# Making pp @ w_in of chunks 2 to 7 one batch at a time, split by ScalarE and VectorE from PSUM

## The chip, the cores and the metric

The kernel runs on one core of a Trainium2 chip. The time is the device time of one execution in microseconds, the median of several runs. A second, profiled execution is read for the reasons; its own time is given beside the runs.

## What is computed

Four batches of 8 heads with 576 rows go through an attention over 32 packed rows, and its result (2304 rows of 512) through two feed-forward stages. q, k, v and p are float32; the weights arrive as float64 and are converted to float32 on the chip.

```python
p_packed = sm_attn(p, k, v)                  # 32 rows per head
out = sm_attn(q, p_packed, p_packed)         # 576 rows per head
x = out as (4*576, 512)
h = x @ w_in;  g = softplus(h);  y = g @ w_out          # d_ff = 2048
z = (sigmoid(y @ w_gate) * (y @ w_val)) @ w_out2        # d_ff = 1536
```

## The kernel before

The attention's second product and the first feed-forward product are joined: a2 (the 576 x 32 softmax of q against the packed rows, per head) times the packed rows pp times w_in is a2 @ (pp @ w_in). So for each batch b and each chunk c of 256 columns of w_in the kernel makes Wp[b, c] = pp @ w_in once, a matrix of 256 x 256 (as 128 partitions x 2 x 256), and then multiplies a2 with it. There are 8 chunks and 4 batches.

Products of full precision are made in two parts: hi is a float32 rounded to the format that TensorE multiplies fast, lo is the remainder x - hi. `mm3` multiplies hi x hi, hi x lo and lo x hi. So every operand has to be split: a copy to hi (`hi_of`, on ScalarE or GpSimd) and a subtraction for lo (`split_lo`, on VectorE or GpSimd). Wp is split into tiles wph and wpl.

For each (b, c) and each half s of the 576 rows, `emit_h` makes h in twelve matmuls of 288 columns into PSUM (lines 111 to 113), ScalarE makes softplus of it (g, L634), the split gives ghl, and two steps later `emit_out1` multiplies it with w_out: four blocks m of six matmuls each (L662, L663, L665), each block into a PSUM bank of its own, which VectorE adds into xa (L670). Chunks 0 and 1 are done batch by batch beside the attention; from chunk 2 on the entries go in pairs of batches (0, 1) and (2, 3).

Preparations are generators in a queue, `jobs`. Between two blocks m a `tick` runs the first job up to its next `yield`. So a job with many yields is spread over many blocks, and what stands behind it in the queue comes later. The queue holds, for each pair of batches, the job that makes the next pair's Wp, and behind it the conversions of w_in and w_out for a later chunk (`prep_win`, `prep_wo`), one early operand of the second stage, and near the end the operands A and B of the second stage (`prep_A`, `prep_B`). `finish` runs the queue until a named job is done. The framework then orders the instructions of each engine.

Wp is made by two functions. `prep_wp_one(b, c)` serves chunks 0 and 1: for one batch four matmuls with 64 columns of bdT (the packed rows as a block-diagonal matrix) as weights, each into one half of the partitions of a bank; ScalarE copies the bank to wph and VectorE subtracts into wpl; one yield. `prep_wp_two(half, c)` serves chunks 2 to 7: for two batches two times two matmuls with 128 columns of bdT. Each of its two banks holds one half of the partitions of both batches, so ScalarE copies it in two halves into float32 tiles of the pool cv (L598), and GpSimd then makes wph (L102) and wpl (L99). For the first pair alone (chunk 2, batches 0 and 1) ScalarE and VectorE split from PSUM in halves (L601). The job has ten yields (eight for the first pair).

The banks of `bank1` come from a pool of four, shared by the blocks of `emit_out1`, the sets of Wp and the conversions.

Of the kernel before, what the change touches and what calls it, by code (L numbers as in the profile page):

```python
# [12 lines left out]
AF = mybir.ActivationFunctionType  # L13
# [7 lines left out]
def attn_moe_moe_kernel(  # L21
# [21 lines left out]
    nc = tc.nc  # L43
# [45 lines left out]
    def bank1():  # L89
        return ps_o[-1].tile([P, 512], F32, tag="o", name="ps1")  # L90
# [7 lines left out]
    def split_lo(eng, lo, x, hi):  # L98
        eng.tensor_tensor(lo, x, hi.bitcast(F32), op=ALU.subtract)  # L99

    def pool_hi(hi, x):
        nc.gpsimd.tensor_scalar(hi, x, 1.0, 0.0, op0=ALU.mult, op1=ALU.add)  # L102

    def hi_of(on_act, hi, x):
        if on_act:
            nc.scalar.activation(hi, x, AF.Copy)  # L106
        else:
            pool_hi(hi, x)
# [23 lines left out]
    for c in range(NCH1):  # L132
        order += [("in", c, f) for f in range(2)] + [("out", c, f) for f in range(2)]
        if c > ECS:
            n = -(-len(early) // (NCH1 - c))
# [110 lines left out]
    jobs = deque()  # L246
# [3 lines left out]
    def tick():  # L250
        for todo_ in (jobs, idle):
            while todo_:
                if next(todo_[0][1], "end") != "end":
                    return
                todo_.popleft()

    def finish(name):
        while any(nm == name for nm, _ in jobs):
            tick()
# [6 lines left out]
    bdT = ph1.tile([P, 2 * B + 2, P], F32, name="bdT")  # L266
# [19 lines left out]

    BLANK = 2
    NWORK = 7
    WPP = 1
    WPH = 0  # L290
    SPL = []
    SP0 = []
    ALO = [['A22'], ['A22', 'S2', 'S4'], ['A22'], ['A22']]
# [214 lines left out]
    def att_left(u):  # L508

        return sum(STAGES - n for _, n, x in live if x <= u) + STAGES * sum(  # L510
            x <= u for x in units
        )

    def att_done(u):
        return att_left(u) == 0
# [6 lines left out]
    def att_tick(last=2 * B):  # L522

        if units and ready(units[0], 0) and units[0] <= last and (
            not live or (len(live) < (NLV if last < 8 else 2) and min(x[1] for x in live) >= (G0 if len(live) == 1 and last < 8 else GP if last < 8 else GAP))
        ):
            u = units.popleft()
            live.append([attn_unit(u), 0, u])
        for x in live:
            if ready(x[2], x[1]):  # L530
                live.remove(x)
                next(x[0])
                x[1] += 1
                if x[1] < STAGES:
                    live.append(x)
                return


    w_in_f, wo_hl, Wp = {}, {}, {}
# [6 lines left out]
    def prep_win(c):  # L546
        wt = ph1.tile([P, KD, CF], F32, tag="w_in", bufs=2, name="w_in")
        for f in range(2):
            yield from convert(("in", c, f), wt[:, :, f * P : (f + 1) * P])
            yield  # L550
        w_in_f[c] = wt

    def prep_wo(c):
        for f in range(2):
            wo_hl[c, f] = yield from convert_split(("out", c, f), wo_p, [P, DM], "wo", 4)
            yield

    def wp_tiles():
        return [
            ph1.tile([P, 2, CF], F32R, tag="wp" + y, bufs=4, name="wp" + y) for y in "hl"  # L560
        ]

    def prep_wp_one(b, c):
        half, odd = divmod(b, 2)
        wt = w_in_f[c]
        hi, lo = wp_tiles()
        ps = bank1().rearrange("p (t n) -> p t n", t=2)
        for t in range(2):
            for par in range(2):
                r = slice(64 * (odd ^ par), 64 * (odd ^ par) + 64)  # L570
                nc.tensor.matmul(
                    ps[r, t, :], bdT[:, 4 * half + 2 * t + par, r], wt[:, 2 * t + par, :],
                    start=True, stop=True,
                )
        nc.scalar.activation(hi, ps, AF.Copy)
        split_lo(nc.vector, lo, ps, hi)
        Wp[b, c] = (hi, lo)
        yield

    def prep_wp_two(half, c):  # L580
        wt = w_in_f[c]
        hl = [wp_tiles() for _ in range(2)]

        far = WPP and (half, c) != (0, 2)
        if far:
            xs = [new_cv().rearrange("p (t n) -> p t n", t=2) for _ in range(2)]
        for par in range(2):
            ps = bank1().rearrange("p (t n) -> p t n", t=2)
            for t in range(2):
                j = 2 * t + par  # L590
                nc.tensor.matmul(  # L591
                    ps[:, t, :], bdT[:, 4 * half + j, :], wt[:, j, :], start=True, stop=True
                )
            yield
            for e in range(2):
                r = slice(64 * e, 64 * e + 64)
                if far:
                    nc.scalar.activation(xs[e ^ par][r], ps[r], AF.Copy)  # L598
                else:
                    hi, lo = hl[e ^ par]  # L600
                    nc.scalar.activation(hi[r], ps[r], AF.Copy)  # L601
                    split_lo(nc.vector, lo[r], ps[r], hi[r])
                yield
            yield
        if far:
            for (hi, lo), x in zip(hl, xs):
                hi_of(WPH, hi, x)
                split_lo(nc.gpsimd, lo, x, hi)
                yield
        for x in range(2):  # L610
            Wp[2 * half + x, c] = hl[x]

    gt, late = {}, deque()

    def split_g(b, c, s, g32):
# [57 lines left out]
    def between(m, att_ticks):  # L673
        if m == LATE and late:
            late.popleft()()
        if m > 0:
            for _ in range(att_ticks[m - 1]):
                att_tick()
        tick()
# [90 lines left out]
    def new_cv():  # L770
        return cv.tile([P, DM], F32, tag="cv", name="cv")
# [41 lines left out]
    def prep_early(fs):  # L813
        for f in fs:
            yield from blocks(f)
            yield
# [31 lines left out]
    n = 0  # L848
# [19 lines left out]
    for i, (b, c) in enumerate(entries):  # L868
        if c == 0:
            while not att_done(2 * b + 1):  # L870
                att_tick()
            if b:
                for cc in range(2):
                    jobs.appendleft((f"wp{b}{1 - cc}", prep_wp_one(b, 1 - cc)))
        if (b, c) == (3, 0):
            jobs.append(("win2", prep_win(2)))
        if (b, c) == (3, 1):
            jobs.append(("wp02", prep_wp_two(0, 2)))
        if c >= 2 and b % 2 == 0:
            k = groups.index((b // 2, c))  # L880
            if k == 0:
                jobs.append(("wo2", prep_wo(2)))
            if k + 1 < len(groups):
                x, cc = groups[k + 1]
                jobs.append((f"wp{2 * x}{cc}", prep_wp_two(x, cc)))
            if k + 2 < len(groups) and weights and groups[k + 2][1] == weights[0]:
                cc = weights.popleft()
                jobs.extend(idle)
                idle.clear()
                jobs.append((f"win{cc}", prep_win(cc)))  # L890
                jobs.append((f"wo{cc}", prep_wo(cc)))
                idle.append((f"early{cc}", prep_early(early_in.get(cc, ()))))
            if (b, c) == BAT:
                jobs.extend(idle)
                idle.clear()
                jobs.append(("B00", prep_B(0, 0)))
        for x in range(2):
            if (b, c) == (x + 2, NCH1 - 2):
                jobs.append((f"A{x}", prep_A(x)))
        if (b, c) == CPC:  # L900
            cps[0] = CPS > 0
        if (b, c) == (1, 2):
            att.release()
            w2.append(tc.alloc_tile_pool(name="w2", bufs=1, side="right"))
        finish(f"wp{b}{c}" if c < 2 else f"wp{b - b % 2}{c}")
        for s in range(2):
            emit_h(b, c, s)
            pace = 0
            for bb in range(b + 1, B if c < 2 else 0):
                slots = 3 * (4 * bb - 2 * i - s) - MARGIN  # L910
                pace = max(pace, -(-att_left(2 * bb + 1) // max(1, slots)))
            ticks = [pace] * 3
            if len(pend) == DEPTH:
                emit_out1(*pend.popleft(), ticks)
            else:
                for m in range(KD):
                    between(m, ticks)
            pend.append((b, c, s))
# [176 lines left out]
```

## Time and profile before

| | us |
|---|---|
| median of 3 runs | 866.27 (866.12 to 866.31) |
| profiled execution, its own time | 866.7 |
| its span | 864.9 |
| TensorE busy | 840.2 |
| VectorE busy | 586.3 |
| GpSimd busy | 475.3 |
| ScalarE busy | 340.0 |

A page of the profile names engines as PE (TensorE matmul), PEld (TensorE weight load), DVE (VectorE), ACT (ScalarE), POOL (GpSimd) and SP (the queue of DMAs). Matmuls are pipelined: a record's duration is longer than the distance to the next one, so the cost of a matmul is read from the distance between starts. A matmul in float32 that isn't split, as those of Wp, leaves two records.

### The profile page before, as it was taken

The page shows a single profiled execution, that of the slowest core. Times are in us where ns is not written, and L with a number is a line of the kernel's source. Part 1 is how long each engine was busy: PE and PEld are TensorE (multiplying, and loading weights), DVE is VectorE, ACT ScalarE, POOL GpSimd, SP SyncE. Part 2 cuts the span into 40 slices and gives each one's busy share as a digit, 9 for nine tenths or more (in the row PEclk, how much of TensorE's full clock was granted, in tenths as well). Part 3 has the DMA queues.
Part 4 walks back from the last instruction along what each step waited for, and adds up shares of the span by engine and source line. Part 5 has one row for each costly group of instructions (what it writes and reads, how often), then busy time and mean ns, then how long its engine had stood idle before and what let it go on. Part 6 is the DMA issues. An engine that isn't in the chain of part 4 may idle for free.

```text
span 864.9 us, 15497 instructions
## 1 busy us (share of the span) xinstructions
PE 840.2 (97%) x6100; PEld 790.1 (91%) x6100; DVE 586.3 (68%) x1003; ACT 340.0 (39%) x626; POOL 475.3 (55%) x453
## 2 busy tenths in 40 slices
PE   6899999999999999999889999999999999999997
PEld 5788999899999999999889999999988999999995
DVE  1876556946465556546788688898896746767665
ACT  4567565554343434454333431232352432322210
POOL 4454333245656545585669787876983734536400
PEclk9999999999999999999999999999999999999999
DMA  9993330203033302300064555644415413213003
GB/s 230 221 223 89 83 80 5 88 11 99 5 96 103 123 25 77 125 26 1 1 198 148 166 168 153 192 129 131 161 56 153 113 47 86 67 44 110 14 1 109
DMA packets 58007, 85.53 MB, mean 99 GB/s; under 512 B 6352, under 2 KB 39248, under 8 KB 57936
## 3 DMA queue, kind: packets, MB, share of 16 engines
q1 hardware_dynamic: 56928, 83.31, 34.3%
q10 hardware_dynamic: 1008, 1.25, 0.4%
q8 instruction: 48, 0.79, 0.4%
q14 instruction: 23, 0.19, 0.1%
HBM read 65.67 MB, written 18.87 MB: 98 GB/s over the span
## 4 chain that ended last, share of the span: by engine, by line
PE 79%; DVE 8%; DMA 6%; ACT 2%; POOL 2%; issue 2%; SPq 0%; POOLq 0%; DVEq 0%; ACTq 0%
PE bank L113 9%; PE bank L111 8%; PE bank L112 8%; PE ps L662 7%; PE ps L663 6%; PE ps L665 6%; PE ps L1010 5%; PE ps L1012 5%; PE ps L1011 5%; PE ps L111 4%; PE ps L113 3%; PE ps L112 3%; DMA xa<-in_k_dram 2%; PE ps L591 2%; PE ps L466 1%
## 5 line engine op out<-in xcount | busy, mean ns | idle before, releaser
L111 PE MATMUL bank<-aop,BH 128*128 128x288 f32 x672 | 199.0, 296 | 4.3 <-ACT work L992 1.1
L113 PE MATMUL bank<-aop,BL 128*128 128x288 f32 x672 | 198.7, 296 | 0.0
L112 PE MATMUL bank<-aop,BH 128*128 128x288 f32 x672 | 197.8, 294 | 0.2 <-DVE aop L99 0.2
L670 DVE TENSOR_TENSOR xa<-xa,ps 128x288 f32<-128x288 f32 x224 | 100.2, 452 | 104.9 <-PE ps L665 104.5
L99 POOL TENSOR_TENSOR ghl<-g,ghl 128x576 fp32r<-128x576 f32 x64 | 93.3, 1458 | 134.2 <-ACT ghl L106 124.8
L662 PE MATMUL ps<-ghl,woh 128*128 128x288 f32 x512 | 148.7, 305 | 2.9 <-DVE xa L670 2.6
L663 PE MATMUL ps<-ghl,wol 128*128 128x288 f32 x512 | 143.4, 295 | 0.0
L111 PEld LDWEIGHTS bank<-aop,BH 128*128 128x128 f32 x672 | 126.2, 188 | 9.9 <-issue 2.1
L112 PEld LDWEIGHTS bank<-aop,BH 128*128 128x128 f32 x672 | 126.4, 188 | 4.2 <-DVE aop L99 0.4
L113 PEld LDWEIGHTS bank<-aop,BL 128*128 128x128 f32 x672 | 126.5, 188 | 0.1
L99 POOL TENSOR_TENSOR BL<-cv,BH 128x512 fp32r<-128x512 f32 (+1 forms) x96 | 118.3, 1249 | 3.5 <-ACT BH L106 2.4
L665 PE MATMUL ps<-ghl,woh 128*128 128x288 f32 x512 | 108.9, 294 | 0.0
L662 PEld LDWEIGHTS ps<-ghl,woh 128*128 128x128 f32 x512 | 96.2, 188 | 5.7 <-ACT aop L725 2.1
L663 PEld LDWEIGHTS ps<-ghl,wol 128*128 128x128 f32 x512 | 96.3, 188 | 0.6
L963 DVE TENSOR_TENSOR work<-work,bank 128x576 f32<-128x576 f32 (+1 forms) x100 | 70.8, 725 | 30.8 <-PE bank L113 29.9
L1010 PE MATMUL ps<-oh,gv 128*128 128x512 f32 x216 | 84.5, 391 | 1.1 <-DVE xa L1018 0.6
L1011 PE MATMUL ps<-ol,gv 128*128 128x512 f32 x216 | 84.9, 393 | 0.0
L1012 PE MATMUL ps<-oh,gv 128*128 128x512 f32 x216 | 84.8, 393 | 0.0
L665 PEld LDWEIGHTS ps<-ghl,woh 128*128 128x128 f32 x512 | 82.2, 188 | 0.0
L1018 DVE TENSOR_TENSOR xa<-xa,ps 128x512 f32<-128x512 f32 x90 | 61.6, 684 | 28.9 <-PE ps L1012 28.4
L111 PE MATMUL ps<-A2h,wph 128*128 128x288 f32 x256 | 77.3, 302 | 0.1
L102 POOL TENSOR_SCALAR BH<-cv 128x512 fp32r<-128x512 f32 (+1 forms) x48 | 28.1, 596 | 88.9 <-PE bank L112 88.7
(128 smaller groups left out, 1633.8 us busy)
## 6 DMA issues: line engine op xcount, KB each, us to landing
cv<-B SPq DMA_DIRECT2D x52, 256.0 KB, 2.7
B<-cv SPq DMA_DIRECT2D x48, 256.0 KB, 3.4
raw_in<-in_moe_w_in_dram SPq DMA_DIRECT2D x16, 512.0 KB, 3.8
raw_out<-in_moe_w_out_dram SPq DMA_DIRECT2D x16, 512.0 KB, 3.6
raw_g<-in_moe_w_gate_dram SPq DMA_DIRECT2D x12, 512.0 KB, 4.2
raw_v<-in_moe_w_val_dram SPq DMA_DIRECT2D x12, 512.0 KB, 4.4
raw_o<-in_moe_w_out_dram SPq DMA_DIRECT2D x12, 512.0 KB, 4.1
xa<-in_q_dram SPq DMA_DIRECT2D x6, 576.0 KB, 6.8
```

What stands on the lines that cost most here:

```text
L99: eng.tensor_tensor(lo, x, hi.bitcast(F32), op=ALU.subtract)
L111: nc.tensor.matmul(ps, wh, xh, start=first, stop=False)
L112: nc.tensor.matmul(ps, wh, xl, start=False, stop=False)
L113: nc.tensor.matmul(ps, wl, xh, start=False, stop=last)
L662: nc.tensor.matmul(out_, wh[:, ms], gh[:, f], start=f == 0, stop=False)
L663: nc.tensor.matmul(out_, wl[:, ms], gh[:, f], start=False, stop=False)
L665: nc.tensor.matmul(out_, wo_hl[c, f][0][:, ms], gl[:, f], start=False, stop=f == 1)
L670: nc.vector.tensor_tensor(dst, dst, out_, op=ALU.add)
L963: nc.vector.tensor_tensor(to, x, y, op=ALU.add)
L1010: nc.tensor.matmul(bank, gh[:, ts_], oh, start=f == 0, stop=False)
L1011: nc.tensor.matmul(bank, gh[:, ts_], ol, start=False, stop=False)
L1012: nc.tensor.matmul(bank, gl[:, ts_], oh, start=False, stop=f == 1)
```

## The change

For chunks 2 to 7 too, Wp is made by `prep_wp_one`, two jobs per pair. `prep_wp_two` and its two switches go. The split is then made by ScalarE and VectorE from PSUM, GpSimd has no part in it, and the float32 tiles in cv go. Each pair has two yields in the queue where it had ten.

```diff
--- before.py
+++ after.py
@@ -286,8 +286,6 @@
 
     BLANK = 2
     NWORK = 7
-    WPP = 1
-    WPH = 0
     SPL = []
     SP0 = []
     ALO = [['A22'], ['A22', 'S2', 'S4'], ['A22'], ['A22']]
@@ -577,39 +575,6 @@
         Wp[b, c] = (hi, lo)
         yield
 
-    def prep_wp_two(half, c):
-        wt = w_in_f[c]
-        hl = [wp_tiles() for _ in range(2)]
-
-        far = WPP and (half, c) != (0, 2)
-        if far:
-            xs = [new_cv().rearrange("p (t n) -> p t n", t=2) for _ in range(2)]
-        for par in range(2):
-            ps = bank1().rearrange("p (t n) -> p t n", t=2)
-            for t in range(2):
-                j = 2 * t + par
-                nc.tensor.matmul(
-                    ps[:, t, :], bdT[:, 4 * half + j, :], wt[:, j, :], start=True, stop=True
-                )
-            yield
-            for e in range(2):
-                r = slice(64 * e, 64 * e + 64)
-                if far:
-                    nc.scalar.activation(xs[e ^ par][r], ps[r], AF.Copy)
-                else:
-                    hi, lo = hl[e ^ par]
-                    nc.scalar.activation(hi[r], ps[r], AF.Copy)
-                    split_lo(nc.vector, lo[r], ps[r], hi[r])
-                yield
-            yield
-        if far:
-            for (hi, lo), x in zip(hl, xs):
-                hi_of(WPH, hi, x)
-                split_lo(nc.gpsimd, lo, x, hi)
-                yield
-        for x in range(2):
-            Wp[2 * half + x, c] = hl[x]
-
     gt, late = {}, deque()
 
     def split_g(b, c, s, g32):
@@ -875,14 +840,16 @@
         if (b, c) == (3, 0):
             jobs.append(("win2", prep_win(2)))
         if (b, c) == (3, 1):
-            jobs.append(("wp02", prep_wp_two(0, 2)))
+            for y in range(2):
+                jobs.append((f"wp{y}2", prep_wp_one(y, 2)))
         if c >= 2 and b % 2 == 0:
             k = groups.index((b // 2, c))
             if k == 0:
                 jobs.append(("wo2", prep_wo(2)))
             if k + 1 < len(groups):
                 x, cc = groups[k + 1]
-                jobs.append((f"wp{2 * x}{cc}", prep_wp_two(x, cc)))
+                for y in range(2):
+                    jobs.append((f"wp{2 * x + y}{cc}", prep_wp_one(2 * x + y, cc)))
             if k + 2 < len(groups) and weights and groups[k + 2][1] == weights[0]:
                 cc = weights.popleft()
                 jobs.extend(idle)
@@ -902,7 +869,7 @@
         if (b, c) == (1, 2):
             att.release()
             w2.append(tc.alloc_tile_pool(name="w2", bufs=1, side="right"))
-        finish(f"wp{b}{c}" if c < 2 else f"wp{b - b % 2}{c}")
+        finish(f"wp{b}{c}")
         for s in range(2):
             emit_h(b, c, s)
             pace = 0
```

TensorE, around a pair in the middle of the stage, before (ps_3365 is the first bank of the pair, woh and wol are w_out's parts):

```order
L665 MATMUL ps_3351<-ghl,woh 128x288 x2
L591 MATMUL ps_3365<-w_in,bdT 128x256 x2
L662 MATMUL ps_3368<-ghl,woh 128x288
L663 MATMUL ps_3368<-ghl,wol 128x288
L662 MATMUL ps_3368<-ghl,woh 128x288
L663 MATMUL ps_3368<-ghl,wol 128x288
L665 MATMUL ps_3368<-ghl,woh 128x288 x2
L662 MATMUL ps_3377<-ghl,woh 128x288
```

And in the changed kernel, at the same place (its lines L627, L628 and L630 are L662, L663 and L665 of before, L569 is L571):

```order
L630 MATMUL ps_3356<-ghl,woh 128x288 x2
L569 MATMUL ps_3366<-w_in,bdT 64x256 x4
L627 MATMUL ps_3373<-ghl,woh 128x288
L628 MATMUL ps_3373<-ghl,wol 128x288
L627 MATMUL ps_3373<-ghl,woh 128x288
L628 MATMUL ps_3373<-ghl,wol 128x288
L630 MATMUL ps_3373<-ghl,woh 128x288 x2
L569 MATMUL ps_3383<-w_in,bdT 64x256 x4
L627 MATMUL ps_3390<-ghl,woh 128x288
```

Before, one set of two matmuls of 128 columns stood between two blocks, and the pair's second set came several blocks later. Now a set of four matmuls of 64 columns stands there, one block behind it the second, and blocks on both sides.

VectorE at that place, before (ps_3351 and ps_3368 are the blocks around the first set):

```order
L187 SCALAR_TENSOR_TENSOR ps_3306<-raw_v,ps_3306 128x512
L670 TENSOR_TENSOR xa<-xa,ps_3323 128x288
L670 TENSOR_TENSOR xa<-xa,ps_3351 128x288
L670 TENSOR_TENSOR xa<-xa,ps_3368 128x288
L670 TENSOR_TENSOR xa<-xa,ps_3377 128x288
L670 TENSOR_TENSOR xa<-xa,ps_3389 128x288
```

And in the changed kernel (L635 is L670 of before; ps_3366 and ps_3383 are the banks of the two sets):

```order
L635 TENSOR_TENSOR xa<-xa,ps_3356 128x288
L99 TENSOR_TENSOR wpl<-ps_3366,wph 128x512
L635 TENSOR_TENSOR xa<-xa,ps_3373 128x288
L178 TENSOR_SCALAR ps_3402<-raw_in 128x512
L99 TENSOR_TENSOR wpl<-ps_3383,wph 128x512
L635 TENSOR_TENSOR xa<-xa,ps_3390 128x288
L183 SCALAR_TENSOR_TENSOR ps_3402<-raw_in,ps_3402 128x512
L635 TENSOR_TENSOR xa<-xa,ps_3405 128x288
```

Before, VectorE only adds blocks here, as GpSimd made wpl. Now a subtraction stands between the additions for each of the two sets, and a conversion of w_in has moved up to here.

GpSimd at the end of the stage, before (aop are the A operands of the second stage, oh and ol belong to its B operands):

```order
L99 TENSOR_TENSOR aop<-xa,aop 128x576
L102 TENSOR_SCALAR oh<-cv 128x512
L99 TENSOR_TENSOR ol<-cv,oh 128x512
L99 TENSOR_TENSOR aop<-sum,aop 128x576
L99 TENSOR_TENSOR ghl<-g_5171,ghl 128x576
L99 TENSOR_TENSOR aop<-sum,aop 128x576
L99 TENSOR_TENSOR ghl<-g_5228,ghl 128x576
L99 TENSOR_TENSOR BL<-cv,BH 128x512
```

And in the changed kernel:

```order
L99 TENSOR_TENSOR ghl<-g_5049,ghl 128x576
L99 TENSOR_TENSOR aop<-sum,aop 128x576
L102 TENSOR_SCALAR oh<-cv 128x512
L99 TENSOR_TENSOR aop<-sum,aop 128x576
L99 TENSOR_TENSOR ol<-cv,oh 128x512
L99 TENSOR_TENSOR ghl<-g_5106,ghl 128x576
L99 TENSOR_TENSOR ghl<-g_5163,ghl 128x576
L99 TENSOR_TENSOR ghl<-g_5213,ghl 128x576
L99 TENSOR_TENSOR BL<-cv,BH 128x512
```

Of the three last A operands that GpSimd makes, the last one stood one ghl before the end; now three ghl come behind it.

## Rows read from the trace of the kernel before

**Rows 1.** The page: span, and busy time by engine.

```profile
span 864.9 us, 15497 instructions
PE 840.2 (97%) x6100; PEld 790.1 (91%) x6100; DVE 586.3 (68%) x1003; ACT 340.0 (39%) x626; POOL 475.3 (55%) x453
```

**Rows 2.** Windows, 178 to 425 us: busy us and instructions by engine, clock, DMA.

```profile
core 0: us, PE busy (x) PEld busy (x) DVE busy (x) ACT busy (x) POOL busy (x), PEclk, DMA share, GB/s
178.00:425.00 247.00, 246.37 (x1803) 243.09 (x1801) 142.14 (x276) 105.79 (x167) 142.04 (x120) 1.00 0.19 60
```

**Rows 3.** Waits of TensorE, 178 to 425 us: total us, times, longest.

```profile
PE ps L662 <- DVE xa L670: 0.2, 1, 0.2
...
PEld ps L662 <- DVE xa L670: 0.8, 2, 0.5
```

**Rows 4.** Timeline of PE, old set: start, us, what, count.

```profile
213.93 1.03 PE L591 MATMUL ps<-w_in,bdT 128*128 128x256 f32 x4
214.61 0.48 PE L111 MATMUL ps<-A2h,wph 128*128 128x288 f32 x1
214.93 0.30 PE L112 MATMUL ps<-A2l,wph 128*128 128x288 f32 x1
215.07 0.29 PE L113 MATMUL ps<-A2h,wpl 128*128 128x288 f32 x1
```

**Rows 5.** Timeline of PE, a set of the new kind in chunk 0.

```profile
56.68 1.08 PE L571 MATMUL ps<-w_in,bdT 128*64 128x256 f32 x8 [0.17 <-ACT qT L357]
57.69 0.40 PE L662 MATMUL ps<-ghl,woh 128*128 128x288 f32 x1
57.93 0.29 PE L663 MATMUL ps<-ghl,wol 128*128 128x288 f32 x1
```

**Rows 6.** Timeline of PE, from 128 to 64 columns of weights.

```profile
61.49 0.29 PE L112 MATMUL ps<-A2l,wph 128*128 128x288 f32 x1
61.62 0.29 PE L113 MATMUL ps<-A2h,wpl 128*128 128x288 f32 x1
61.84 0.54 PE L441 MATMUL ps<-a1T,xa 96*64 96x32 f32 x12
```

**Rows 7.** Timeline of PE, two new sets back to back.

```profile
153.83 1.95 PE L571 MATMUL ps<-w_in,bdT 128*64 128x256 f32 x16
155.71 0.40 PE L111 MATMUL ps<-A2h,wph 128*128 128x288 f32 x1
155.94 0.30 PE L112 MATMUL ps<-A2l,wph 128*128 128x288 f32 x1
```

**Rows 8.** Groups, 178 to 425 us: busy us, mean ns, idle before.

```profile
L670 DVE TENSOR_TENSOR xa<-xa,ps 128x288 f32<-128x288 f32 x188 | 84.5, 452 | 95.7 <-PE ps L665 95.4
...
L99 POOL TENSOR_TENSOR wpl<-cv,wph 128x512 fp32r<-128x512 f32 x22 | 28.6, 1322 | 0.0
L598 ACT ACTIVATE cv<-ps 64x512 f32<-64x512 f32 x44 | 26.1, 592 | 15.3 <-PE ps L591 14.7 <-POOL cv L791 0.3
...
L102 POOL TENSOR_SCALAR wph<-cv 128x512 fp32r<-128x512 f32 x22 | 13.8, 646 | 7.0 <-ACT cv L598 7.0
```

**Rows 9.** Tile wph, 30 to 160 us (ns min/median/max), and VectorE's waits there.

```profile
L575 ACT ACTIVATE wph<-ps x8: 597/598/600, 40.0 to 155.8; 128x512 fp32r<-128x512 f32 x8
L99 DVE TENSOR_TENSOR wpl<-ps,wph x8: 671/684/693, 40.9 to 157.7; 128x512 fp32r<-128x512 f32 x8
...
DVE wpl L99 <- ACT wph L575: 4.4, 4, 2.6
```

**Rows 10.** Timeline of PE, 424 to 429 us: the two waits.

```profile
425.11 0.40 PE L662 MATMUL ps<-ghl,woh 128*128 128x288 f32 x1 [0.44 <-DVE xa L670]
...
428.86 0.37 PE L662 MATMUL ps<-ghl,woh 128*128 128x288 f32 x1 [1.91 <-DVE xa L670]
```

**Rows 11.** Timeline of VectorE, same stretch.

```profile
422.72 1.97 DVE L699 TENSOR_TENSOR sum<-xa,sum 128x576 f32<-128x576 f32 x1 [1.85 <-POOL aop L99]
424.61 0.81 DVE L670 TENSOR_TENSOR xa<-xa,ps 128x288 f32<-128x288 f32 x2
427.00 0.76 DVE L699 TENSOR_TENSOR sum<-xa 128x576 f32<-128x576 f32 x1 [1.58 <-POOL aop L99]
```

**Rows 12.** Timeline of GpSimd, same stretch.

```profile
421.26 1.43 POOL L99 TENSOR_TENSOR aop<-sum,aop 128x576 fp32r<-128x576 f32 x1
422.64 1.43 POOL L99 TENSOR_TENSOR ghl<-g,ghl 128x576 fp32r<-128x576 f32 x1
425.54 1.43 POOL L99 TENSOR_TENSOR aop<-sum,aop 128x576 fp32r<-128x576 f32 x1 [1.47 <-ACT aop L725]
```

## Prediction

> **What bounds the kernel now.** I read the page first: TensorE is busy for 840.2 of 864.9 us [rows 1]. A share over the whole span says little about one stage, so I cut out the stretch that the change lies in. The columns c = 2 to 7 of the first product run from about 178 us to about 425 us, and one call over that stretch shows TensorE busy for 246.37 of 247.00 us at a granted clock of 1.00, the level of 2.4 GHz, while VectorE has 142.14, GpSimd 142.04 and ScalarE 105.79 us of work in it [rows 2]. The waits of the stretch say the same from the other side: TensorE's matmuls waited once, for 0.2 us, on VectorE's additions into xa, and its weight loads 0.8 us in two waits on the same [rows 3]. GpSimd and the wph and wpl that it makes end no wait of TensorE there. So in this stretch a nanosecond taken from GpSimd, ScalarE or VectorE buys nothing, and a nanosecond of TensorE's time is a nanosecond of the kernel's. The question to ask of the change is what it does to TensorE's stream, and only then whether VectorE's new work makes TensorE wait.
>
> **The change part by part.**
>
> *TensorE.* Both versions make 24 sets of products pp @ w_in in this stretch (12 pairs of batches, two sets each). A set before is two matmuls with 128 columns of weights, which the trace shows as four records; a set now is four matmuls with 64 columns, alternating between the two halves of the output partitions, eight records. The streamed columns are the same 256. The trace has both kinds, because c = 0 and 1 already use the function that the change now uses everywhere.
>
> A set of the old kind: it starts at 213.93, the next matmul at 214.61, the one behind it at 214.93, and from there the usual distance holds (215.07, that is 0.13 to 0.14 us) [rows 4]. From 213.93 to 214.93 is 1.00 us, in which one ordinary matmul of 0.13 went too: the set costs 0.87 us.
>
> A set of the new kind: it starts at 56.68, the next matmul at 57.69, the second at 57.93 [rows 5]. That is 1.25 us less 0.13, or 1.12 us. The tail is the difference: behind the old set the next weight load was already done, behind the new one TensorE stands for a moment before matmuls of 128 columns come at their usual distance. There is a price in front as well, which this row hides, since its set started after a wait. I read it at another place where an ordinary matmul is followed by one with 64 columns of weights: 61.62 to 61.84, 0.22 us in place of 0.13 [rows 6], so 0.09 us more. Together a set that stands alone costs 1.21 us, 0.34 us above the old one.
>
> Do the new sets stand alone? In the new order one output block of six matmuls lies between the two sets of a pair, in all 12 pairs, and such a block stands before the first and behind the second too. So the price is paid 24 times: 24 x 0.34 = 8.2 us, all on the path that sets the end.
>
> The Trainium skill says in TensorEngine Tiling (Array Packing), under Key Properties, that a change of tiling mode, as distinct from a change of tile, drains TensorE. By it the price belongs to the switch and not to the matmul, and two sets side by side should pay it once. A pair of sets back to back in this trace agrees: 16 records take from 153.83 to 155.94, 2.11 less 0.13, so 1.98 us and not 2 x 1.12 [rows 7]. Counted by the switch the sum is 8.2 us; counted by the matmul, from half of that pair, it would be 4.0, and that is the first rival below.
>
> *ScalarE* loses 44 copies of half the partitions at 592 ns (26.0 us) and gets copies of all partitions at 598 ns, at most 24 (14.4 us) [rows 8, 9]. *GpSimd* loses 22 copies of 646 ns and 22 subtractions of 1322 ns, 43.3 us [rows 8]. Neither engine ends a wait of TensorE in the stretch, so I book both at nothing; TensorE's full row of matmuls is the cover.
>
> *VectorE* gets at most 24 subtractions at 684 ns, 16.4 us [rows 9], on top of 142.14 in 247 us. That is 64% of the stretch, so it isn't short of time. But each subtraction waits for ScalarE's copy, and behind it in VectorE's queue stand the additions of 452 ns [rows 8] that free the PSUM banks for TensorE. There are four banks. In the new order a set takes a bank, the block behind it another, the second set a third, the next block the fourth, and the block after that wants the bank of the first set again, or, where a conversion of weights has taken that one, the bank of the first of these blocks. From the end of the first set to that point TensorE has a block (6 x 0.13), a set (1.21) and a block: 2.8 us. In that time the copy (0.60), the subtraction (0.68) and one addition (0.45) have to run, 1.73 us. About 1.0 us is left over, and the price is nothing as long as ScalarE takes the set up within that. The nearest row for how late it can be is c = 0 and 1, where VectorE waited for this copy in 4 of 8 cases, 4.4 us in all, 2.6 at most [rows 9]. At the worst, 1.6 us over in one of eight sets, that is 3 x 1.6 = 4.8 us. From below it can't be less than nothing, as hardly a wait is there to be removed. That counts the whole of the longest wait as lateness, though it holds the copy's own 0.60. I take 0: the mean of the four waits is 1.1 us, 0.5 without the copy, which is within the slack. The 4.8 stays for the range.
>
> *The job queue.* A pair took ten ticks of the queue and now takes two. What stands behind it (the conversions of w_in and w_out, the first B operand, the A operands) moves forward, so their DMAs on SP's queue are issued earlier relative to the blocks; their order on that queue stays but for one load of raw_v that goes behind one load of B. None of them ends a wait of TensorE in the stretch. One thing late in the stage can gain: TensorE waited 0.44 us at 425.11 and 1.91 us at 428.86 for VectorE's additions [rows 10], which stood behind a sum for the A operands that waited for GpSimd and once took 1.97 us itself instead of 0.76 [rows 11]; GpSimd had a ghl of the main stream between two of these operands [rows 12]. In the new order the last A operands come before the last three ghl instead of the last one, and GpSimd has no wph to make. The gain lies between nothing (the same chain of waits, only earlier) and all 2.35 us. I take 1.0, near the middle as the chain itself stays.
>
> **The sum.** +8.2 - 1.0 = +7.2 us. The profiled execution took 866.7 us by its own clock, 864.9 of it span, and lies 0.4 above the median of the runs, 866.27. On the profiled one that is 873.9, on the median 873.5. From some thirty rows behind the last set on, TensorE's order is the same in both versions, so I expect no difference in the second half.
>
> **The rivals.**
>
> *The price goes by the matmul.* Then two sets side by side or apart cost the same: 0.99 + 0.05 for half a front, 1.04 us, 0.17 above the old, 24 x 0.17 = 4.0 us, and 866.3 + 4.0 - 1.0 = 869.3. For it speaks only that one row has no isolated set without a wait ahead of it; against it that the tail behind 8 and behind 16 records is equal [rows 5, 7].
>
> *A new wait takes over.* VectorE holds TensorE up through the banks, as worked out: 866.3 + 8.2 + 4.8 - 1.0 = 878.3. It decides once ScalarE is more than 1.0 us late with a set. ScalarE's load speaks against it (105.79 of 247 us, and it gets less).
>
> *The other side: faster.* The switch costs nothing in this stretch because the queue of TensorE is full and weights come ahead, and the earlier A operands remove the waits at 425.11, 428.86 and the 0.2 us of the stretch: 866.3 - 2.6 = 863.7. It decides if a new set costs less than 0.87 + 2.6/24 = 0.98 us. Against it: ordinary matmuls were queued behind the set at 56.68 as well, and it still paid.
>
> **How the numbers follow.** The forecast has 0.78, the price by the matmul 0.07, the new wait 0.10, the faster case 0.05. The forecast alone ranges from 871.5 to 875.5 (all or none of the 2.6 us regained, and a microsecond of small waits). With the two slower rivals as ends, the range is 869.2 to 878.4. About 0.2% (1.7 us) is what a measurement of this kernel can tell from no change. Of the faster case 0.04 falls below that, 0.01 within it; I add 0.01 for a regain larger than I found. That leaves 0.94 for slower.
>
> **What would show it.** In the profile of the changed kernel the sets should stand 1.2 us from the last matmul before to the second behind, less the ordinary ones, in all 24 places, with TensorE's weight load idle before the next block. GpSimd's busy time should fall by some 43 us and ScalarE's by 12 to 14, with no gain from it. VectorE should show some 14 to 16 us more. The second half should be as long as before, only later. A set at 0.9 us would prove me wrong on the size, and waits of TensorE on the additions above 3 us in the stretch would prove me wrong on the banks.

## The result and the profile after

The changed kernel takes 872.38 us, the median of four runs (870.72 to 873.32), against 866.29 for the kernel before (866.12 to 866.67). The ratio is 1.0059, with a 95% interval of 1.0043 to 1.0074: slower, by 6.1 us in the medians. Its profiled execution took 870.72 us against 866.7, so the traces have 4.0 us to explain. Part of the difference between 6.1 and 4.0 is spread: in a later comparison the eight runs of the changed kernel with a granted clock of 0.999 or more lie between 870.46 and 871.97, and four below that at 877.1 to 881.4; at 0.999 or more the medians there are 871.36 and 866.58 us, 4.8 apart.

In the changed kernel the lines have other numbers: L569 and L573 are the matmuls and the copy of `prep_wp_one` (L571, L575 before), L627, L628, L630 and L635 are L662, L663, L665 and L670 of before, and L664 and L690 are L699 and L725.

The page of the changed kernel, span and busy time by engine, answers to [rows 1]:

```profile
span 868.9 us, 15631 instructions
PE 848.4 (98%) x6196; PEld 785.2 (90%) x6196; DVE 597.4 (69%) x1023; ACT 325.6 (37%) x602; POOL 432.3 (50%) x409
```

GpSimd has 43.0 us less to do and ScalarE 14.4 less, and the span grew by 4.0. TensorE is busy 8.2 us longer. The windows of the changed kernel, with the columns of [rows 2], over the same stretch and over the second half, and then the second half of the kernel before:

```profile
178.00:425.00 247.00, 246.81 (x1840) 231.40 (x1839) 149.69 (x290) 90.28 (x141) 95.47 (x73) 1.00 0.20 60
441.18:868.90 427.72, 419.52 (x2664) 389.05 (x2664) 320.12 (x453) 125.49 (x214) 255.79 (x253) 1.00 0.38 111
```

```profile
436.43:864.90 428.47, 419.53 (x2664) 388.95 (x2664) 320.66 (x454) 125.44 (x214) 257.49 (x254) 1.00 0.38 111
```

In the stretch TensorE's matmuls are still without a gap (246.81 of 247.00 us), at the same clock; the engine for weights has fallen from 243.09 to 231.40 us. That is the mark of the new sets: the loads stand still around them. The timeline of TensorE in the changed kernel (start, duration, what, count) shows the two sets of a pair with a block between them:

```profile
245.80 0.43 PE L630 MATMUL ps<-ghl,woh 128*128 128x288 f32 x2
246.16 1.08 PE L569 MATMUL ps<-w_in,bdT 128*64 128x256 f32 x8
247.18 0.40 PE L627 MATMUL ps<-ghl,woh 128*128 128x288 f32 x1
247.41 0.29 PE L628 MATMUL ps<-ghl,wol 128*128 128x288 f32 x1
...
248.17 1.08 PE L569 MATMUL ps<-w_in,bdT 128*64 128x256 f32 x8
```

From one set to the next it is 2.01 us. A block of six matmuls is 6 x 0.133 = 0.80, which leaves 1.21 for a set. The parts can be read too: the two matmuls from 245.80 would let the next one start 0.27 later, and the set starts 0.36 later (0.09 in front); from its start to the second matmul behind it is 1.25, less one matmul of 0.13 (1.12). Read so from the starts of all records, each of the 24 sets costs 1.207 to 1.212 us, 29.0 together; before, 23 of the 24 cost 0.856 to 0.868 and one 1.07, 20.9 together.

The same stretch on the engine for weights, in the changed kernel (in brackets the idle time ahead and what ended it):

```profile
246.16 0.63 PEld L569 LDWEIGHTS ps<-w_in,bdT 128*64 128x64 f32 x8 [0.17 <-issue]
247.17 0.19 PEld L627 LDWEIGHTS ps<-ghl,woh 128*128 128x128 f32 x1 [0.39 <-DVE ps L178]
```

The load of the next block comes 0.39 us after the last load of the set, shortly before the set's last matmul ends (246.16 + 1.08 = 247.24, a modelled end). Behind an old set, in the kernel before, it followed at once:

```profile
213.80 0.76 PEld L591 LDWEIGHTS ps<-w_in,bdT 128*128 128x128 f32 x4
214.58 0.19 PEld L111 LDWEIGHTS ps<-A2h,wph 128*128 128x128 f32 x1
```

The releaser in the bracket of the changed kernel (a conversion on VectorE) must not be believed here. The waits of the weight engine between 178 and 425 us (total us, times, longest) show why:

```profile
PEld ps L627 <- DVE xa L635: 7.0, 18, 0.4
...
PEld ps L627 <- DVE ps L178: 0.4, 1, 0.4
```

The same 0.39 us comes again behind one set after the other, under whatever name came last: 7.0 in 18 is 0.39 each, and 0.4 is the longest. TensorE's waits for other engines in these traces vary in length (0.19 to 1.91 us); this one doesn't.

The waits of TensorE's matmuls, 160 to 442 us, and the two ends of the stage in the changed kernel:

```profile
PE ps L627 <- DVE xa L635: 0.6, 2, 0.4
```

```profile
167.77 1.08 PE L569 MATMUL ps<-w_in,bdT 128*64 128x256 f32 x8
...
431.76 0.40 PE L627 MATMUL ps<-ghl,woh 128*128 128x288 f32 x1 [0.45 <-DVE xa L635]
...
441.18 0.40 PE L111 MATMUL bank<-aop,BH 128*128 128x288 f32 x1 [0.55 <-DVE xa L635]
```

and the same two ends in the kernel before, where the view ends ahead of the first set's fourth record:

```profile
168.35 0.81 PE L591 MATMUL ps<-w_in,bdT 128*128 128x256 f32 x3
...
436.43 0.40 PE L111 MATMUL bank<-aop,BH 128*128 128x288 f32 x1 [1.01 <-DVE xa L670]
```

The 1.91 us wait of [rows 10] is gone, and so is half of a wait of 1.01 where the second stage begins, which the prediction had not listed. Before, the matmuls waited 0.24 + 0.44 + 1.91 + 1.01 = 3.6 us from the first set to the second stage; now 0.19 + 0.45 + 0.55 = 1.2. The balance: from the first set to the second stage the trace has 268.1 us before and 273.4 after, +5.3: the sets bring +8.1, the stops, measured between the starts of matmuls, took 5.2 us before and 2.3 after, -2.9 (the waits themselves are -2.4 of it), and +0.1 has no name. Up to the first set it is -0.6, and the second half takes 427.72 in place of 428.47, -0.75, with the same matmuls. Together +4.0.

At the end of the stage, GpSimd and VectorE in the changed kernel, which answer to [rows 12] and [rows 11]:

```profile
422.70 1.43 POOL L99 TENSOR_TENSOR aop<-sum,aop 128x576 fp32r<-128x576 f32 x1
424.10 0.62 POOL L102 TENSOR_SCALAR oh<-cv 128x512 fp32r<-128x512 f32 x1
426.12 1.44 POOL L99 TENSOR_TENSOR aop<-sum,aop 128x576 fp32r<-128x576 f32 x1 [1.41 <-ACT aop L690]
427.51 1.31 POOL L99 TENSOR_TENSOR ol<-cv,oh 128x512 fp32r<-128x512 f32 x1
428.76 5.26 POOL L99 TENSOR_TENSOR ghl<-g,ghl 128x576 fp32r<-128x576 f32 x3
```

```profile
424.16 1.16 DVE L664 TENSOR_TENSOR sum<-xa,sum 128x576 f32<-128x576 f32 x1 [1.49 <-POOL aop L99]
...
427.60 1.84 DVE L664 TENSOR_TENSOR sum<-xa 128x576 f32<-128x576 f32 x1 [1.55 <-POOL aop L99]
```

VectorE still waits 1.5 us for GpSimd twice, but the last of these sums now lies 13.6 us ahead of the second stage, where before it lay 9.4 ahead (427.00 of [rows 11] against 436.43), and three ghl follow on GpSimd.

The subtractions of the changed kernel, 160 to 440 us (ns min/median/max, first and last), and VectorE's waits for ScalarE's copy, 160 to 441 us (total us, times, longest), answer to [rows 9]:

```profile
L99 DVE TENSOR_TENSOR wpl<-ps,wph x24: 676/691/694, 170.9 to 399.7; 128x512 fp32r<-128x512 f32 x24
```

```profile
DVE wpl L99 <- ACT wph L573: 16.2, 19, 1.2
```

VectorE waited for ScalarE's copy in 19 of 24 sets, 16.2 us in all, and not a matmul waited for the banks because of it.

### The profile page after: what moved, and what is told of

The parts are those of the page before. It is cut to its first block, busy times and chain, and to the rows that moved or that the text cites. A ratio compares the mean times of both kernels' runs of the same rounds, so it can differ in the third digit from the quotient of the medians.

```text
span 868.9 us, 15631 instructions
## 1 busy us (share of the span) xinstructions
PE 848.4 (98%) x6196; PEld 785.2 (90%) x6196; DVE 597.4 (69%) x1023; ACT 325.6 (37%) x602; POOL 432.3 (50%) x409
## 3 DMA queue, kind: packets, MB, share of 16 engines
q10 hardware_dynamic: 1008, 1.25, 0.4%
## 5 line engine op out<-in xcount | busy, mean ns | idle before, releaser
L635 DVE TENSOR_TENSOR xa<-xa,ps 128x288 f32<-128x288 f32 x224 | 99.6, 450 | 80.9 <-PE ps L630 80.0
L627 PE MATMUL ps<-ghl,woh 128*128 128x288 f32 x512 | 147.6, 303 | 0.8 <-DVE xa L635 0.6
L628 PE MATMUL ps<-ghl,wol 128*128 128x288 f32 x512 | 143.5, 295 | 0.0
L630 PE MATMUL ps<-ghl,woh 128*128 128x288 f32 x512 | 109.4, 295 | 0.1
L627 PEld LDWEIGHTS ps<-ghl,woh 128*128 128x128 f32 x512 | 96.2, 188 | 11.3 <-DVE xa L635 7.6
L628 PEld LDWEIGHTS ps<-ghl,wol 128*128 128x128 f32 x512 | 96.5, 188 | 0.1
L630 PEld LDWEIGHTS ps<-ghl,woh 128*128 128x128 f32 x512 | 82.2, 188 | 0.3 <-POOL ghl L99 0.3
L113 PE MATMUL ps<-A2h,wpl 128*128 128x288 f32 x256 | 76.1, 297 | 0.4 <-DVE wpl L99 0.4
```

Of the source, the lines that this page charges most:

```text
L113: nc.tensor.matmul(ps, wl, xh, start=False, stop=last)
L627: nc.tensor.matmul(out_, wh[:, ms], gh[:, f], start=f == 0, stop=False)
L628: nc.tensor.matmul(out_, wl[:, ms], gh[:, f], start=False, stop=False)
L630: nc.tensor.matmul(out_, wo_hl[c, f][0][:, ms], gl[:, f], start=False, stop=f == 1)
L635: nc.vector.tensor_tensor(dst, dst, out_, op=ALU.add)
```

## Experiments

The reading that the price goes with the switch of weight width is called S; its rival lets the price go with each narrow matmul, or with the engines that split. For the waits at the end of the stage, Q says that the fewer ticks of the queue took them away, G that GpSimd's relief did. The first four kernels ran beside a kernel before of 867.30 us (29 runs), the other three beside 866.49 (21 runs).

| kernel | us | ratio (95%) |
|---|---|---|
| changed_again | 871.88 | 1.0074 (1.0050 to 1.0099) |
| sets_side_by_side | 868.55 | 1.0030 (1.0009 to 1.0051) |
| wide_sets_split_from_psum | 863.46 | 0.9965 (0.9952 to 0.9978) |
| narrow_sets_split_by_gpsimd | 874.26 | 1.0077 (1.0061 to 1.0093) |
| changed_ten_ticks | 875.46 | 1.0093 (1.0075 to 1.0112) |
| before_two_ticks | 867.40 | 1.0020 (0.9999 to 1.0041) |
| wide_sets_two_ticks | 870.27 | 1.0056 (1.0037 to 1.0076) |

**changed_again**: the changed kernel, unedited, as the base of its comparison.

> The changed kernel once more, beside the others of this call. Both theories: 872.4 us. A second profile shows whether the 24 sets cost 1.21 us each again (theory S, the switch of TensorE between weights of 128 and of 64 columns) and which waits of TensorE differ where its runs spread from 870.7 to 873.3.

It took 871.88 us, and its profile (871.97) has the same 1.207 to 1.212 us for each set and the same waits, but for the one of 0.19, which is 0.11 here. What differs is the second half, in the columns of [rows 2]:

```profile
441.70:870.18 428.48, 420.13 (x2664) 388.91 (x2664) 320.52 (x453) 125.35 (x214) 255.03 (x253) 1.00 0.37 111
```

It took 427.72 us in the first profile of the same program and 428.47 in the kernel before. So a difference of 0.75 us there is one that a single program shows against itself. This second profile is 5.3 us longer than that of the kernel before, and from the first set to the second stage it is 5.5 longer (273.6 against 268.1): all of the difference lies in the stage that the change touches.

**sets_side_by_side**: the changed kernel with the two sets of a pair back to back.

```diff
+    def prep_wp_pair(x, c):
+        for y in range(2):
+            next(prep_wp_one(2 * x + y, c))
+        yield
...
-                for y in range(2):
-                    jobs.append((f"wp{2 * x + y}{cc}", prep_wp_one(2 * x + y, cc)))
+                jobs.append((f"wp{2 * x}{cc}", prep_wp_pair(x, cc)))
...
```

> The changed kernel with both sets of a pair made in one tick, so that they stand side by side on TensorE: 12 places in chunks 2 to 7 instead of 24. Theory S (the price is paid once per switch): 12 x 0.34 = 4.1 us below the changed kernel, 868.3. Theory M (the price goes by the matmul): as the changed kernel, 872.4. Theory W (VectorE's split from PSUM holds TensorE up): two sets at once fill two banks, 872.4 or more.

868.55 us, 3.3 below the changed kernel. TensorE's timeline in this kernel at a pair, and where it waited:

```profile
245.92 0.43 PE L635 MATMUL ps<-ghl,woh 128*128 128x288 f32 x2
246.28 1.95 PE L569 MATMUL ps<-w_in,bdT 128*64 128x256 f32 x16
248.16 0.40 PE L632 MATMUL ps<-ghl,woh 128*128 128x288 f32 x1
248.40 0.30 PE L633 MATMUL ps<-ghl,wol 128*128 128x288 f32 x1
```

```profile
172.86 0.40 PE L632 MATMUL ps<-ghl,woh 128*128 128x288 f32 x1 [1.16 <-DVE wpl L99]
```

From 246.28 to 248.40 less 0.13, and 0.09 in front: a pair costs 2.08 us by these rows (2.07 by the records), not 2 x 1.21 = 2.42. Twelve pairs take 24.9 us, 4.1 below the changed kernel, and the new wait of 1.16 us at 172.86 takes some back: -3.0 by the trace, -3.3 measured. The same matmuls with half the switches have half the price, so S holds. The wait is of the kind that the prediction had as a rival (two sets in a row hold two of the four banks until VectorE has subtracted); of the twelve pairs only the first has it.

**narrow_sets_split_by_gpsimd**: the kernel before with the new matmuls alone; copies, GpSimd's split and the ten ticks stay.

```diff
-                j = 2 * t + par
-                nc.tensor.matmul(
-                    ps[:, t, :], bdT[:, 4 * half + j, :], wt[:, j, :], start=True, stop=True
-                )
+                for par in range(2):
+                    r = slice(64 * (odd ^ par), 64 * (odd ^ par) + 64)
+                    nc.tensor.matmul(
+                        ps[r, t, :], bdT[:, 4 * half + 2 * t + par, r], wt[:, 2 * t + par, :],
+                        start=True, stop=True,
+                    )
...
```

> The kernel before with its ticks, its copies to cv and its split by GpSimd, but with sets of four matmuls of 64 columns for one batch. Theory S: 866.3 + 24 x 0.34 = 874.5, and no wait of the end of the stage is regained. Theory W: VectorE has nothing new to do, so 866.3.

874.26 us, +7.0 on the kernel before. TensorE's timeline in this kernel, a set and the wait at the end of the stage:

```profile
252.57 1.08 PE L592 MATMUL ps<-w_in,bdT 128*64 128x256 f32 x8
253.59 0.40 PE L664 MATMUL ps<-ghl,woh 128*128 128x288 f32 x1
253.82 0.29 PE L665 MATMUL ps<-ghl,wol 128*128 128x288 f32 x1
...
437.46 0.37 PE L664 MATMUL ps<-ghl,woh 128*128 128x288 f32 x1 [1.91 <-DVE xa L672]
```

The set is that of the changed kernel to a hundredth, though GpSimd splits; and the 1.91 us wait is there. So the price comes with the narrow sets alone, and the regain with something else. A narrow set has weights of 64 columns and each matmul's output in half of the partitions; no run parts these two. The time fits S's 874.5 partly by luck: in the profiled execution (875.6) the granted clock was 0.50 from 438.89 to 442.30 us, behind the 1.91 us wait, which cost some 1.5 us, and against the kernel before of its own comparison the runs are 7.0 longer and not 8.2.

**wide_sets_split_from_psum**: the other half. The sets stay wide, ScalarE and VectorE split all of them from PSUM as they did the first pair. With that a pair has eight ticks, where it had ten.

```diff
-    WPP = 1
+    WPP = 0
```

> The kernel before with its sets of 128 columns, but ScalarE and VectorE split every pair from PSUM in halves, as they do for the first pair; GpSimd has no part. Theory S: no switch, so no price; 866.3 less what GpSimd's relief gives back, 0 to 2.6 us, that is 863.7 to 866.3. Theory W: VectorE has 44 more subtractions of 0.68 us between its additions, more than in the changed kernel, so 872.4 or more.

863.46 us: below both kernels, and 0.2 below S's range. TensorE's timeline in this kernel, its waits from 160 to 448 us, and the window of [rows 2]:

```profile
242.52 1.03 PE L591 MATMUL ps<-w_in,bdT 128*128 128x256 f32 x4
243.20 0.48 PE L662 MATMUL ps<-ghl,woh 128*128 128x288 f32 x1
243.52 0.29 PE L663 MATMUL ps<-ghl,wol 128*128 128x288 f32 x1
```

```profile
PE bank L111 <- DVE xa L670: 1.0, 1, 1.0
...
PE ps L662 <- DVE xa L670: 0.5, 2, 0.3
```

```profile
178.00:425.00 247.00, 246.75 (x1811) 244.20 (x1812) 170.29 (x321) 106.65 (x168) 101.28 (x77) 1.00 0.19 60
```

The set costs 0.87 as before, and 28 us more of VectorE's work (142.14 to 170.29) brings TensorE no wait but one of 0.25 at 421.91. The waits up to the second stage are 1.5 us in place of 3.6. That is 2.1 of the 4.0 by which its profiled execution (862.67) lies below that of the kernel before; of the other 1.9, 0.5 lie ahead of the first set and 0.8 in the second half (427.71 us), about as much as the two profiles of the changed kernel differ by there, and the rest has no name. At the end of the stage VectorE's timeline answers to [rows 11]:

```profile
419.43 1.97 DVE L699 TENSOR_TENSOR sum<-xa,sum 128x576 f32<-128x576 f32 x1 [2.21 <-POOL aop L99]
421.32 1.53 DVE L670 TENSOR_TENSOR xa<-xa,ps 128x288 f32<-128x288 f32 x4
423.72 0.76 DVE L699 TENSOR_TENSOR sum<-xa 128x576 f32<-128x576 f32 x1 [0.86 <-POOL aop L99]
```

Both sums still wait for GpSimd, and GpSimd has its last two A operands, each with one ghl behind it, as in the kernel before. But four additions stand between the two sums and not two, and TensorE waits 0.26 us there in place of 1.91.

**changed_ten_ticks**: the changed kernel with as many ticks per pair as before, five for each set.

```diff
+    def prep_wp_slow(b, c):
+        yield from prep_wp_one(b, c)
+        for _ in range(4):
+            yield
...
```

> The changed kernel with four empty yields behind each set, so that a pair takes ten ticks of the queue as before. It tells where the waits at the end of the stage went (0.44 and 1.91 us before; 0.44 and 1.91 again with narrow sets split by GpSimd; 0.45 in the changed kernel). Theory Q (the queue's fewer ticks bring the A operands forward): the wait of 1.9 us is back, some 2 us above the changed kernel, 874. Theory G (GpSimd has no wph and wpl to make, so its part of the A operands comes in time): as the changed kernel, 872, with waits at the end of the stage of at most 0.6 us.

875.46 us. The wait is back, though GpSimd makes no wph. TensorE's waits in this kernel and its timeline behind the second one, and the windows of four microseconds around the wait and 3.4 behind it:

```profile
295.95 0.40 PE L632 MATMUL ps<-ghl,woh 128*128 128x288 f32 x1 [1.73 <-DVE xa L640]
...
438.68 0.37 PE L632 MATMUL ps<-ghl,woh 128*128 128x288 f32 x1 [1.91 <-DVE xa L640]
...
440.64 0.44 PE L632 MATMUL ps<-ghl,woh 128*128 128x288 f32 x1
440.88 0.44 PE L633 MATMUL ps<-ghl,wol 128*128 128x288 f32 x1
```

```profile
436.00:440.00 4.00, 2.09 (x16) 1.89 (x16) 3.18 (x7) 1.26 (x2) 1.84 (x2) 1.00 0.02 4
440.00:443.40 3.40, 3.40 (x16) 3.40 (x16) 3.28 (x7) 0.63 (x1) 1.59 (x2) 0.50 0.24 25
```

So Q holds against G: GpSimd's relief alone doesn't take the wait away. Two things went beyond what Q had foreseen. The clock stood at 0.50, the level of 1.2 GHz, for 3.4 us behind the wait, with matmuls 0.24 us apart in place of 0.13; some 13 of them cost 1.4 us. And the wait of 1.73 us at 295.95 is new, no other kernel here has it: VectorE's addition stood behind a conversion that had waited 3.2 us for a load of raw_in.

**before_two_ticks**: the kernel before with two ticks per pair; GpSimd still splits.

```diff
-            yield
             for e in range(2):
...
-                yield
             yield
...
                 split_lo(nc.gpsimd, lo, x, hi)
-                yield
```

> The kernel before (sets of 128 columns, split by GpSimd) with two yields per pair instead of ten. Theory Q: the wait of 1.9 us at the end of the stage goes, 864.4. Theory G: it stays, 866.3. If both had a part, GpSimd's 43 us of wph and wpl come in bunches earlier and the wait shrinks in part, 865.3.

867.40 us, 0.9999 to 1.0041 of the kernel before: no gain that can be told, where Q had 864.4. The waits of TensorE in this kernel, 160 to 430 us, and the one at the end of the stage:

```profile
PE ps L659 <- ACT cv L597: 0.9, 1, 0.9
...
PE ps L659 <- DVE xa L96: 0.6, 1, 0.6
```

```profile
425.61 0.40 PE L659 MATMUL ps<-ghl,woh 128*128 128x288 f32 x1 [0.45 <-DVE xa L667]
```

The 1.91 us wait is gone with the ticks, as Q said. In its place there are two waits for banks, a new one of 0.9 on ScalarE's copies and one of 0.6 on VectorE, which was 0.13 in the kernel before. The profiled execution took 864.72 us, but the median shows no gain; that step of Q isn't shown.

**wide_sets_two_ticks**: both together, wide sets, split from PSUM, two ticks.

```diff
-    WPP = 1
+    WPP = 0
...
-            yield
             for e in range(2):
...
-                yield
             yield
```

> Sets of 128 columns, split by ScalarE and VectorE from PSUM, two yields per pair: the changed kernel in all but the width of the sets and the split in halves. Theory S: 24 x 0.35 = 8.3 us below the changed kernel, 863.5 to 864. If ScalarE's and VectorE's doubled split, now in two places close together, holds the banks: up to 24 x 0.2 = 4.8 us more than that, 868.

870.27 us: a miss. It is 6.8 above wide_sets_split_from_psum, which ran in the other comparison. The waits of the weight engine in this kernel, 178 to 438 us:

```profile
PEld ps L659 <- DVE xa L667: 3.3, 7, 1.0
```

wide_sets_split_from_psum has no wait on xa there. From the first set to the second stage it is 271.0 us against 265.3: +5.7. The weight engine's waits overlap matmuls, so they can't be counted as lost time; measured between the starts of matmuls, the stops outside the sets took 7.6 us in place of 2.9, which is 4.7 of the 5.7. Another +1.8 lies in the second half, where I found no cause. A wide set needs four operations to give a bank back, two copies and two subtractions of half the partitions. With one tick between the sets, they and the conversions meet in the banks. That the banks are the reason for all 5.7 is argued, not shown.

## Why the prediction was right

**The price of a set.** 24 x 0.34 = 8.2 us was forecast, 8.1 measured. Reading it from chunk 0 and adding the front from another place gave 1.21 us, and all 24 sets show 1.21. One reading was loose: behind the old set the next weight load was not already done, it followed the set's last load at once (214.58), where behind a new set it came 0.39 us later. That it goes with the visit and not with the matmul is shown by sets_side_by_side, that it goes with nothing of the new split by the pair narrow_sets_split_by_gpsimd (the price without the new split) and wide_sets_split_from_psum (the new split without the price). The rival by the matmul had 4.0 us here and is out.

The rule of the Trainium skill in TensorEngine Tiling (Array Packing), Key Properties, that a change of the tiling mode drains TensorE, agrees with 2.07 us for a pair in one visit against 2 x 1.21 in two.

**The engines relieved.** GpSimd 43.0 less (43.3 forecast) and ScalarE 14.4 less (12 to 14, so a little more), and neither ended a wait of a matmul of 0.1 us or more in the stretch, before or after. One weight load had waited 0.3 us for ScalarE's wph at the first pair before, which the prediction left out.

**VectorE and the banks.** The forecast of no cost held, though VectorE stood waiting for the copy in 19 of 24 sets, 1.2 us at most. The copy's own 0.60 is in that, so the lateness was 0.6, within the 1.0 that the working had allowed. VectorE's busy time rose by 11.1 and not 14 to 16: the subtractions brought 13.8, as the first pair lost its four, and the rest are other operations a little shorter and records that overlap. The rival was no phantom: one tick less between the sets brings 1.16 us (sets_side_by_side), and stops of this kind may be a part of what makes wide_sets_two_ticks slower.

**The regain was mis-sized.** The prediction took 1.0 us, the middle between none and 2.35. It was 2.4 by the waits, and 2.9 with the slow starts next to them: the whole wait of 1.91, and half of a wait of 1.01 where the second stage begins, which it had not counted. It also gave the queue and GpSimd's relief as joint reasons. For the 1.91, changed_ten_ticks and before_two_ticks show that the ticks decide: it is there with ten ticks with or without GpSimd's split, and with two ticks 0.45 is left, either way. How the ticks do it is not shown. The prediction's sign, how many ghl follow the last A operand on GpSimd, is not it: wide_sets_split_from_psum has one behind it as before, and waits 0.26. There four additions lie between VectorE's two sums, so the likelier reading is that it counts where the sums land among the additions; no run was made for that alone. What halved the 1.01 stays open as well: it is 0.55 in the two kernels with narrow sets and ten ticks too, but there the clock had fallen just ahead of it.

**The second half** was forecast equal. It is 0.75 us shorter in the first profile of the changed kernel and as long as before in the second (changed_again), so the forecast holds within what one program differs by from itself. The first profiled execution is 3.2 us below the 873.9 forecast for it: 1.9 is the larger regain, 0.75 the second half, 0.6 the start, 0.1 the sets, and these come to 0.15 too much. The second (871.97) is 1.9 below, about as much as the larger regain alone. In the medians it is 872.38 against 873.5. That the median lies nearer to the forecast than either profile is luck, as the regain was taken at a third of its size and the spread of the runs, which no run here explains, made up for part of it.

## What to carry to other kernels

On a TensorE without gaps, look at what a change does to the width of the weights before looking at the engines that it relieves: each visit from 128 columns to 64 and back cost 0.35 us here, so put narrow sets side by side or keep them wide. Splitting the wide sets from PSUM was worth something (863.46 us, with two ticks less per pair beside it, so GpSimd's relief alone isn't priced), and the narrow sets with which it was done cost more than that. A job's yields decide where everything behind it in the queue lands and how long banks are held; move them one at a time, and look at both ends.

## What was not expected of the hardware

Eight records with 64 columns of weights take no longer than four with 128 (0.86 us each way, once the switch is taken off). The starts of the records show how: the narrow ones come two at a time, 0.007 us apart, with 0.21 to 0.26 us from one pair to the next, and the wide ones come singly, 0.216 us apart. A sum on VectorE of 0.76 us took 1.16 to 1.97 us while GpSimd worked beside it [rows 11]. And behind a wait of 1.91 us TensorE's clock stood at 0.50 for 3.4 us in changed_ten_ticks and in narrow_sets_split_by_gpsimd, but not in the profiled execution of the kernel before, which has the same wait and a clock of 1.00 throughout that stage; what tells them apart is open.
